# A planner's durations: float32 value products at their traced length, and rough durations without a margin from the seventeenth head on

## The chip, the cores and the metric

One core of a Trainium2 chip runs the whole kernel in one launch. The metric is the device time of that launch in microseconds (us); lower is better. The engines are called PE (TensorE), DVE (VectorE), ACT (ScalarE), POOL (GpSimd) and SP (SyncE, which here only issues DMAs).

## What is computed

Three layers stand behind each other, all with float32 results (cut from the reference):

```python
# attention: 4 batches, 8 heads, 576 positions, head size 64
scores = q @ k^T / 8 + min(bias, 0)      # bias from a running sum of max(s, 0); causal
attn   = exp(scores - max);  attn /= sum + 1e-9;  x = attn @ v      # -> 2304 tokens x 512
# first MoE-like layer (w_in, w_out are float64)
h = x @ w_in;  g = h * sigmoid(1.702 * h);  x = g @ w_out           # 512 -> 2048 -> 512
# second layer: 8 experts
P = exp(x @ w_gate - max), rows and columns of P balanced 8 times
out = sum over e of  P[:, e] * (max(x @ w1[e], 0) @ w2[e])          # 512 -> 1024 -> 512
```

## The kernel before

**Stages.** Attention and the first layer run interleaved until about 560 us, the rest of the first layer follows to about 660 us, and the second layer, eight experts over three blocks of 768 tokens, takes all that is left. The change touches what is planned in the first two stretches.

**Attention** goes through 64 heads (a head of the code is one batch, one of 8 heads and one of two ranges of its queries). Each head gives one unit (256 queries in two groups) or three units (groups of 128, 128 and 64 queries), 128 units in all. A unit takes three steps on PE, each behind work of other engines:

- `scores` (line 816): products into the tile `sp`; then DVE adds the mask and takes the least value (`sm<-sp,mask`), and ACT takes the exponential (`sm<-sm,stats`).
- `turn` (line 866): PE transposes (`tp<-ident,sm`); for the first 14 heads (`N_F`) a copy to `pf` follows, later ACT writes a float16 part `ph` and DVE the rest `pl`.
- `values` (line 893): PE multiplies with the values (`op<-vf,pf` in float32 for the first 14 heads, `op<-v,ph` and `op<-v,pl` in float16 afterwards); then `finish` on DVE.

Operands of a later head are prepared by `prep` (line 663): the load `kq`, a cast to `one`, a DMA `two<-one` inside the chip's memory, and two subtractions.

**First layer.** A token block of 256 becomes whole when its heads are finished. For each of 8 weight pairs `mm1` (line 1054) makes 24 products into `hp`, then tanh, a product and a split into `gh` and `gl` on ACT and DVE; `mm2` (line 1076) makes 24 products into `acc` (or `accx`). These are called block products below. They come in groups of 12, and a group depends on little, so it can stand between two steps of attention. The weights are float64 and are loaded (`st`) and split by `convert` (line 1168), on ACT and DVE.

**What sets the order.** Every instruction of the kernel goes through a `Sequencer` (line 61) while the program is built. It keeps a clock for each engine and gives each instruction a planned duration (`cost`, line 138), an extra time until its result counts as there (`op.tail`, in `submit`, line 159), and a time at which its inputs are ready (`depend`, line 199). PE instructions are placed at once; those of the other engines are held and issued in the order in which the planner thinks that they can run (`run`, line 259). `any_copy` (line 479) gives a copy to DVE or ACT, whichever is planned to be less loaded.

The main loop (from line 2034) asks each kind of PE work when its inputs are there (`can_vpow`, `can_flush`, `can_value`, `can_turn`, `can_score`, then the first layer), and takes the first kind in this list that is ready. It asks twice: first with `seq.slack = SLACK`, 1000 ns on top of each input's planned end (`settled`, line 101), so that a step whose inputs are only just there gives way to a block product; and if nothing passes, with 0. Where nothing is ready and the first block product hasn't come yet, `fill` (line 476) puts in products that nobody reads (`unread<-mask`), to keep PE working.

Planned durations of before, in ns, with n the columns: a matmul n / 2.4 (four times this for float32 operands) plus 2.7 or 13 and a weight load that isn't hidden; DVE 66 + n / 0.96 (60 more with a scalar operand from a tile) with a tail of 85; ACT 50 or 90 + n / 1.2 (100 more with such an operand) with a tail of 110. From `begin_second` (line 1888) on, `seq.fine` is set, and other durations hold.

All engine instructions are recorded by one helper, so the profile shows line 307 for nearly everything; tiles tell them apart. `n_pv` counts the heads whose values are prepared; `2 * H` is 16.

## Time and profile before

| | us |
|---|---|
| median of 3 runs (2004.4 to 2006.52) | 2006.13 |
| the profiled execution, its own time | 2004.02 |
| span of that execution, first to last instruction | 2002.3 |
| PE busy in the span | 1964.1 (98%) |
| DVE busy | 1471.9 (74%) |
| ACT busy | 1249.3 (62%) |
| POOL busy | 87.2 (4%) |

The chain that ended last runs through PE for 73% of the span. Busy time of PE includes products that run at the lower of its two clocks, so the granted clock (a share of full speed, by stretch) has to be read beside it. A matmul's duration in the profile has a modelled end; what one costs in a row of equal ones is the distance from start to start. A float32 product (both operands plain float32) is recorded as two matmuls.

### The profile page before, as it was taken

How to read it: one execution, taken by the hardware profiler on the slowest of the kernel's cores; microseconds unless marked ns; L12 is line 12 of the kernel's file. 1: busy time of each engine (PE TensorE's matmuls, PEld its weight loads, DVE VectorE, ACT ScalarE, POOL GpSimd, SP SyncE). 2: the span in 40 equal slices, each digit the busy share in tenths (PEclk: the TensorE clock that was granted, in tenths of full speed). 3: DMA queues.
4: the chain of work that ended last, by engine and by line, in shares of the span. 5: the costliest groups of instructions: out<-in, count | busy, mean ns of one | idle time of the engine just before them, and what ended most of it. 6: DMA issues, size and time to landing. Idle time of an engine off the chain costs nothing.

```text
span 2002.3 us, 41146 instructions
## 1 busy us (share of the span) xinstructions
PE 1964.1 (98%) x15805; PEld 1578.6 (79%) x15805; DVE 1471.9 (74%) x3421; ACT 1249.3 (62%) x2576; POOL 87.2 (4%) x144
## 2 busy tenths in 40 slices
PE   7989999999999999999999999999999999999999
PEld 6888999999998677777777777777777777777777
DVE  7787888887853676988877766776786876777656
ACT  6787667675634575666666666656666666665333
POOL 1000000000000000000000111111101001111000
PEclk9999999999999999999999999999999999999999
DMA  8455455444226454475475566667557556566331
GB/s 253 126 187 176 123 141 155 130 130 118 76 69 213 156 198 151 159 257 182 156 256 145 131 184 176 181 171 203 161 130 244 152 156 181 163 172 182 119 129 43
DMA packets 230100, 322.12 MB, mean 161 GB/s; under 512 B 38272, under 2 KB 156224, under 8 KB 229904
## 3 DMA queue, kind: packets, MB, share of 16 engines
q1 hardware_dynamic: 216944, 295.90, 45.1%
q0 software_dynamic: 12960, 23.60, 8.2%
q8 instruction: 124, 2.03, 0.4%
q14 instruction: 72, 0.59, 0.1%
HBM read 230.85 MB, written 84.34 MB: 157 GB/s over the span
## 4 chain that ended last, share of the span: by engine, by line
PE 73%; DVE 10%; ACT 6%; DMA 2%; issue 1%; SPq 0%; ACTq 0%; DVEq 0%
PE C L307 16%; PE A L307 16%; PE D L307 16%; PE B L307 8%; PE hp L307 6%; PE acc L307 3%; ACT h L307 2%; PE accw L307 2%; DVE h L307 2%; PE op L307 1%; PE sp L307 1%; PE tp L307 1%; DVE hst L307 1%; DVE sa L307 1%; DMA kq<-in_qk_dram 1%
## 5 line engine op out<-in xcount | busy, mean ns | idle before, releaser
L307 PEld LDWEIGHTS <-h 128*128 128x128 f16 x6048 | 591.4, 98 | 85.4 <-issue 6.7
L307 PEld LDWEIGHTS <-w1o 128*128 128x128 f16 x4036 | 394.6, 98 | 255.1 <-issue 4.4
L307 PE MATMUL C<-xt,w1o 128*128 128x384 f16 x1152 | 218.6, 326 | 1.4 <-DVE hst L307 1.4
L307 PE MATMUL D<-xt,w1o 128*128 128x384 f16 x1152 | 218.4, 326 | 0.0
L307 PE MATMUL D<-w2o,h 128*128 128x256 f16 x1728 | 217.7, 273 | 0.2 <-ACT y L307 0.2
L307 PE MATMUL A<-xt,w1o 128*128 128x384 f16 x1152 | 214.8, 326 | 0.1
L307 PE MATMUL A<-w2o,h 128*128 128x256 f16 x1728 | 212.2, 273 | 1.7 <-ACT B L307 1.4
L307 PE MATMUL C<-w2o,h 128*128 128x256 f16 x1728 | 208.4, 273 | 1.9 <-DVE y L307 1.7
L307 DVE SCALAR_TENSOR_TENSOR h<-hst,h 128x768 f16<-128x768 f32 (+1 forms) x192 | 139.1, 755 | 55.9 <-ACT h L307 55.9
L307 ACT COPY C<-B 128x384 f32<-128x384 f32 (+1 forms) x168 | 71.4, 425 | 154.7 <-PE B L307 93.7
L307 PE MATMUL hp<-xh,wih 128*128 128x256 f32 (+1 forms) x512 | 154.4, 302 | 0.8 <-ACT xh L307 0.5
L307 PE MATMUL hp<-xl,wih 128*128 128x256 f32 (+1 forms) x512 | 152.1, 297 | 0.6 <-DVE xl L307 0.6
L307 PE MATMUL hp<-xh,wil 128*128 128x256 f32 (+1 forms) x512 | 151.8, 297 | 0.0
L307 POOL DMA_DIRECT2D acc_d<-y x90 | 77.8, 864 | 1224.4 <-DVE y L307 660.3
L307 ACT ACTIVATE h<-hst 128x768 f16<-128x768 f32 (+1 forms) x192 | 126.2, 678 | 3.8 <-DVE hst L307 3.7
L307 ACT ACTIVATE sm<-sm,stats 64x576 f32<-64x576 f32 (+4 forms) x160 | 93.7, 602 | 41.2 <-DVE stats L307 40.1
L307 PE MATMUL acc<-gh,woh 128*128 128x256 f32 x384 | 112.4, 293 | 0.0
L307 PE MATMUL B<-w2o,h 128*128 128x256 f16 x864 | 110.5, 273 | 0.1
L307 PE MATMUL acc<-gl,woh 128*128 128x256 f32 x384 | 109.9, 286 | 0.0
L307 PE MATMUL acc<-gh,wol 128*128 128x256 f32 x384 | 109.6, 285 | 0.0
L307 PE MATMUL B<-xt,w1o 128*128 128x384 f16 x576 | 109.3, 326 | 0.0
L307 ACT COPY B<-A 128x384 f32<-128x384 f32 (+1 forms) x168 | 70.3, 426 | 59.0 <-PE A L307 58.4
(238 smaller groups left out, 3877.0 us busy)
## 6 DMA issues: line engine op xcount, KB each, us to landing
xt<-xc_d SPq DMA_DIRECT2D x168, 384.0 KB
wm<-in_moe_w_dram SPq DMA_DIRECT2D x112, 256.0 KB
w2o<-w_d SPq DMA_DIRECT2D x56, 512.0 KB
wr<-in_moe_w_dram SPq DMA_DIRECT2D x112, 256.0 KB
w_d<-wo SPq DMA_DIRECT2D x98, 256.0 KB
acc_d<-y POOLq DMA_DIRECT2D x90, 256.0 KB, 4.9
kq<-in_qk_dram SPq DMA_DIRECT2D x32, 448.0 KB
st<-in_moe_w_in_dram SPq DMA_DIRECT2D x16, 512.0 KB
```

Source lines behind the costliest of these rows:

```text
L307: self.seq.submit(self.name, what, lambda: method(*args, **named), outs, ins, "accum_op" in named)
```

## The change

It edits the planner alone; the computation stays what it is, and so do the numbers of its instructions, but for four `fill` products and a few copies that change between DVE and ACT.

- From the program's start: a float32 matmul is planned by the longer of its columns and those of its weights. The float32 value products have 65 columns and 128 (or 64) weight columns, so one goes from 4 * 65 / 2.4 + 2.7 = 111 ns to 4 * 128 / 2.4 + 10 = 223 ns. An ACT `activation` that reads bytes or a strided tile (the weight conversion) is planned 54 columns longer.
- Once `n_pv` reaches 16, `seq.rough` is set, until `seq.fine` takes over: DVE 70 + n / 0.96, ACT 90 + n / 1.2 with no addition for scalar operands, matmuls without the additions and with weight loads at nothing, float32 at 65 columns again, no tail behind DVE and ACT results, and the same waiting time behind an engine's own results as another engine would have. The main loop then asks once, with a slack of 0.
- The summary of the change names low parts on GpSimd. `any_less` (line 486), which makes the low parts, uses DVE in both versions, and GpSimd's rows are the same in both.

```diff
--- before.py
+++ after.py
@@ -79,6 +79,7 @@
         self.rank = 0
         self.holding = False
         self.fine = False
+        self.rough = False
         self.slack = 0
         self.cold, self.since, self.streamed = True, 0.0, 0.0
         self.late = 0.0
@@ -135,9 +136,25 @@
             n *= x
         return n
 
+    @staticmethod
+    def strided(ap):
+        return abs(list(ap.ap)[-1][0]) > 1
+
     def cost(self, engine, what, out, ins, sums=False):
         n = max(self.size(x) for x in [out] + ins[:2])
         psum = any(x.space == PSUM for x in ins)
+        if self.rough and not self.fine:
+            if engine == "PE":
+                n = self.size(out)
+                if what == "transpose":
+                    return 2 * n / 2.4
+                slow = ins[0].dtype == F32 or ins[0].dtype == F32R and n < 256
+                return n * (4 if slow else 1) / 2.4
+            if engine == "DVE":
+                quick = what in ("tensor_copy", "tensor_scalar") and not psum
+                return 70 + n / (1.92 if quick else 0.96)
+            if engine == "ACT":
+                return 90 + n / 1.2 + 190 * sums
         if self.fine:
             if engine == "PE":
                 return self.size(out) * (4 if ins[0].dtype == F32 else 1) / 2.4 + (13 if ins[0].dtype == F32R else 2.7)
@@ -145,13 +162,17 @@
             n = self.size(out)
             if what == "transpose":
                 return 2 * n / 2.4 + 3
-            slow = ins[0].dtype == F32 or ins[0].dtype == F32R and n < 256
+            if ins[0].dtype == F32:
+                return 4 * max(n, self.size(ins[0])) / 2.4 + 10
+            slow = ins[0].dtype == F32R and n < 256
             return n * (4 if slow else 1) / 2.4 + (13 if ins[0].dtype == F32R else 2.7)
         by = any(self.size(x) == 1 for x in ins[1:]) and n > 1
         if engine == "DVE":
             quick = what in ("tensor_copy", "tensor_scalar") and not psum
             return 66 + 60 * by + n / (1.92 if quick else 0.96)
         if engine == "ACT":
+            if what == "activation" and (ins[0].dtype == U8 or self.strided(ins[0])):
+                n += 54
             return (50 if psum else 90) + 100 * by + 93 * sums + n / 1.2
         return 80 + n * {"memset": 0.3, "tensor_scalar": 2.7}.get(what, 2.24)
 
@@ -171,9 +192,11 @@
             op.stream = 0.36 if what == "matmul" and ins[0].dtype == F32 else 1.0
             sums = len(outs) > 1
             if engine == "PE":
-                op.load = 110 if BYTES[ins[0].dtype] == 4 else 27
+                op.load = 0 if self.rough else 110 if BYTES[ins[0].dtype] == 4 else 27
             op.cost = self.cost(engine, what, outs[0], ins, sums)
-            op.tail = {"DVE": 85, "ACT": 110}.get(engine, 0) + 90 * sums
+            op.tail = 0
+            if self.fine or not self.rough:
+                op.tail = {"DVE": 85, "ACT": 110}.get(engine, 0) + 90 * sums
         for ap, writes in [(x, False) for x in ins] + [(x, True) for x in outs]:
             name = ap.tensor.name
             if name in self.outside:
@@ -200,7 +223,7 @@
         if on.end is None:
             op.waits.add(on)
             on.after.append(op)
-        elif on.engine == op.engine != "PE" and not on.nbytes:
+        elif (self.fine or not self.rough) and on.engine == op.engine != "PE" and not on.nbytes:
             op.ready = max(op.ready, on.end + AFTER_OWN)
         elif on.engine != "PE" or op.engine != "PE":
             op.ready = max(op.ready, on.end + LATENCY.get((on.engine, op.engine), LATENCY.get(on.engine, 0)))
@@ -2039,7 +2062,9 @@
         more_scales()
         seq.run()
         now = seq.free["PE"]
-        for seq.slack in (SLACK, 0):
+        if not seq.rough and n_pv >= 2 * H:
+            seq.rough = True
+        for seq.slack in (0,) if seq.rough else (SLACK, 0):
             times = [can_vpow(), can_flush(), can_value(), can_turn(), can_score(), moe1_can()]
             which = next((k for k, x in enumerate(times) if x <= now), None)
         if at_first and seq.share() < SHARE:
```

The instructions move on all engines until about the end of attention; the last 10,658 matmuls of PE (the whole second layer among them) stand in the same order as before. Three places follow; `acc`, `hp`, `sp`, `tp` and `op` are the tiles named above, `vtp` a transposition for the scale of the values, which marks the same point of the program in both.

**PE at the first 8-column `vtp`**, in the last of the float32 heads (heads 11 to 13). Before, from the last block product on:

```order
L307 MATMUL acc_945<-gh,wol_79 128x256
L307 MATMUL vtp<-ident,vmax 8x128
L307 MATMUL tp<-ident,sm 128x64 x5
L307 MATMUL sp<-one_114 64x288
L307 MATMUL sp<-two_115 64x288
L307 MATMUL sp<-one_114 64x288
L307 MATMUL sp<-two_115 64x288
L307 MATMUL tp<-ident,sm 128x128 x3
L307 MATMUL op<-vf_134,pf 64x65
L307 MATMUL op<-vf_135,pf 64x65
L307 MATMUL op<-vf_136,pf 64x65
L307 MATMUL op<-vf_137,pf 64x65
```

After that the list goes on for 142 matmuls (44 transpositions, 24 of scores, 74 of values) without a block product. With the change:

```order
L330 MATMUL hp<-xh,wil_81 128x256
L330 MATMUL op<-vf_134,pf 128x65
L330 MATMUL op<-vf_135,pf 128x65
L330 MATMUL op<-vf_136,pf 128x65
L330 MATMUL op<-vf_137,pf 128x65
L330 MATMUL vtp<-ident,vmax 8x128
L330 MATMUL op<-vf_134,pf 64x65
L330 MATMUL op<-vf_135,pf 64x65
L330 MATMUL op<-vf_136,pf 64x65
L330 MATMUL op<-vf_137,pf 64x65
L330 MATMUL op<-vf_138,pf 64x65
L330 MATMUL tp<-ident,sm 128x128 x7
```

The `vtp` now stands between two groups of 12 `hp` products, with 39 matmuls of attention between the groups (15 transpositions, 8 of scores, 16 of values). In the part ahead of it, three other stretches of attention without a block product or a `fill` are 27, 31 and 37 matmuls long.

**SP's DMA queue between the `two<-one` of head 20 and that of head 21.** Before:

```order
L307 DMA two_113<-one_112 64x256
L307 DMA two_115<-aux_d 4x2x256
L307 DMA va<-in_v_dram 128x128
L307 DMA kq<-in_qk_dram 128x2x256
L307 DMA st<-in_moe_w_in_dram 128x2x512
L307 DMA st<-in_moe_w_out_dram 128x1024
L307 DMA st<-in_moe_w_in_dram 128x2x512
L307 DMA two_113<-aux_d 4x2x256
L307 DMA va<-in_v_dram 128x128
L307 DMA two_115<-one_114 64x256
```

With the change:

```order
L330 DMA two_113<-one_112 64x256
L330 DMA kq<-in_qk_dram 128x2x256
L330 DMA st<-in_moe_w_in_dram 128x2x512
L330 DMA st<-in_moe_w_out_dram 128x1024
L330 DMA two_113<-aux_d 4x2x256
L330 DMA st<-in_moe_w_in_dram 128x2x512
L330 DMA two_115<-one_114 64x256
```

Three loads of weights (`st`) stand between the two in both; two small loads that stood in front of the second `two<-one` have moved elsewhere. On PE, the block products between the last scores of head 19 and the first of head 21 go from 72 to 84, and the value products from 18 to 27. Between heads 24 and 26 the same count of block products falls from 36 to 12.

**PE between the scores and the transpositions of a unit of head 51**, at about 400 us. Before (24 `hp` products stand between):

```order
L307 MATMUL sp<-one_114 128x256
L307 MATMUL sp<-two_115 128x256
L307 MATMUL hp<-xh,wih_1592 128x256
L307 MATMUL hp<-xl,wih_1592 128x256
L307 MATMUL hp<-xh,wil_1593 128x256
...
L307 MATMUL hp<-xl,wih_1592 128x256
L307 MATMUL hp<-xh,wil_1593 128x256
L307 MATMUL tp<-ident,sm 128x128 x3
```

With the change (12 of them):

```order
L330 MATMUL sp<-one_114 128x256
L330 MATMUL sp<-two_115 128x256
L330 MATMUL hp<-xh,wih_1408 128x256
L330 MATMUL hp<-xl,wih_1408 128x256
L330 MATMUL hp<-xh,wil_1409 128x256
...
L330 MATMUL hp<-xl,wih_1408 128x256
L330 MATMUL hp<-xh,wil_1409 128x256
L330 MATMUL tp<-ident,sm 128x128 x3
```

The transposition has come closer to the scores whose exponential it reads. Among the units from 60 to 127, five now have 12 block products there, alone or with two of scores or 9 to 15 of values (1.4 to 2.0 us by the starts of equal products in the trace); before, the least of these five had 12 with 18 of values.

## Rows read from the trace of the kernel before

**Rows 1.** The page: span.

```profile
span 2002.3 us, 41146 instructions
```

**Rows 2.** Windows by stage: from:to, length, busy us (x) of PE, PEld, DVE, ACT, POOL; clock, DMA, GB/s.

```profile
35.00:190.00 155.00, 141.46 (x1206) 129.32 (x1204) 128.71 (x361) 122.90 (x235) 1.31 (x9) 0.93 0.54 166
190.00:560.00 370.00, 363.81 (x3597) 347.82 (x3596) 300.95 (x922) 244.35 (x506) 3.18 (x22) 1.00 0.45 128
560.00:2002.00 1442.00, 1432.87 (x10811) 1080.98 (x10809) 1020.99 (x2056) 861.61 (x1795) 77.80 (x90) 1.00 0.55 167
```

**Rows 3.** The same columns, windows of 5 us in the early stretch.

```profile
75.00:80.00 5.00, 3.72 (x31) 3.44 (x29) 3.96 (x12) 3.14 (x7) 0.00 (x0) 1.00 0.51 120
80.00:85.00 5.00, 5.00 (x30) 4.53 (x28) 3.47 (x9) 2.10 (x3) 0.00 (x0) 0.66 0.67 226
85.00:90.00 5.00, 4.92 (x40) 4.00 (x39) 4.32 (x20) 4.01 (x7) 0.14 (x1) 1.00 0.09 24
90.00:95.00 5.00, 5.00 (x33) 4.17 (x32) 3.46 (x11) 3.38 (x7) 0.14 (x1) 0.66 0.06 14
...
135.00:140.00 5.00, 3.68 (x21) 3.59 (x22) 2.68 (x8) 3.61 (x8) 0.00 (x0) 0.54 0.65 216
140.00:145.00 5.00, 5.00 (x40) 5.00 (x38) 4.00 (x10) 3.33 (x8) 0.00 (x0) 0.78 0.39 94
...
170.00:175.00 5.00, 4.73 (x25) 3.67 (x24) 4.50 (x10) 3.08 (x6) 0.15 (x1) 0.50 0.65 209
```

**Rows 4.** Timeline of PE: start us, us, what [idle before <-releaser].

```profile
84.22 0.29 PE L307 MATMUL acc<-gh,wol 128*128 128x256 f32 x1
...
87.98 0.88 PE L307 MATMUL op<-vf,pf 128*128 128x65 f32 x6
88.67 0.48 PE L307 MATMUL sp<-one 128*128 128x512 f32 x1
...
101.55 0.22 PE L307 MATMUL op<-v,ph 128*128 128x65 f16 x2 [0.93 <-DVE xg L307]
...
103.30 0.20 PE L307 MATMUL op<-v,pl 128*128 128x65 f16 x1 [0.69 <-DVE pl L307]
...
103.89 0.36 PE L307 MATMUL hp<-xh,wih 128*128 128x256 f32 x1
```

**Rows 5.** Waits of PE from 0 to 560 us: us in total, times, longest.

```profile
PE sp L307 <- DMA two<-one: 4.0, 3, 2.9
...
PE op L307 <- DVE pl L307: 2.3, 5, 0.7
...
PE tp L307 <- ACT sm L307: 1.7, 4, 0.9
```

**Rows 6.** Timeline of the DMA queue of SP, 127 to 131 us.

```profile
127.26 0.38 SPq L307 DMA_DIRECT2D st<-in_moe_w_in_dram  x1
...
130.63 0.52 SPq L307 DMA_DIRECT2D two<-one  x1
```

**Rows 7.** Timeline of PE, 132 to 137 us.

```profile
132.22 0.28 PE L307 MATMUL hp<-xl,wih 128*128 128x256 f32 x1
...
133.17 0.28 PE L307 MATMUL sp<-one 128*128 128x256 f32 x1
136.32 0.58 PE L307 MATMUL sp<-two 68*128 68x256 f32 x1 [2.86 <-DMA two<-one]
```

**Rows 8.** ACT by form, 190 to 560 us: xcount | busy us, mean ns | idle before.

```profile
L307 ACT ACTIVATE sm<-sm,stats 128x256 f32<-128x256 f32 x16 | 8.0, 502 | 2.9 <-DVE stats L307 2.9
...
L307 ACT ACTIVATE sm<-sm,stats 128x128 f32<-128x128 f32 x16 | 6.4, 401 | 3.2 <-DVE stats L307 3.1
L307 ACT ACTIVATE va<-va,vpow 128x128 f32<-128x128 f32 x16 | 6.2, 395 | 1.4 <-DVE vpow L307 0.8 <-DMA va<-in_v_dram 0.6
```

**Rows 9.** DVE by form, 190 to 560 us.

```profile
L307 DVE CUSTOM_DVE_ANT_0 sm<-sp,mask 128x256 f32<-128x256 f32 x16 | 6.6, 415 | 0.0
...
L307 DVE CUSTOM_DVE_ANT_0 sm<-sp,mask 128x128 f32<-128x128 f32 x16 | 4.5, 281 | 3.6 <-PE sp L307 2.6 <-PE vtp L307 0.8
```

## The prediction

> **What bounds the kernel now.** The span is 2002.3 us [rows 1]; the profiled execution took 2004.02, 1.7 more for what lies around the span, and stands 2.1 under the median of 2006.13. I read the windows by stage first [rows 2]: what TensorE lacks of a window's length is its idle time. From 35 to 190 us it is 155.0 - 141.5 = 13.5 us, from 190 to 560 us 370.0 - 363.8 = 6.2, from 560 on 1442.0 - 1432.9 = 9.1. So TensorE is the bound everywhere, and a new order of the same products can only win or lose idle time and time at the lower clock. The last 10,658 matmuls keep their order, so from about 560 us on I count nothing.
>
> Next come the windows of 5 us [rows 3]. A granted clock of 0.66 over 5 us means that 0.34 of the window was lost, 1.7 us, since the clock has only its two levels, full speed and half (2.4 and 1.2 GHz). After 35 us it falls four times: in 80 to 85 (1.7 lost), in 90 to 95 (1.7), in 135 to 145 (5 x 0.46 + 5 x 0.22 = 3.4) and from 170 on (2.5 in the window shown). From 190 us on it is at 1.00 [rows 2]. Idle and clock together put about 25 us at stake between 35 and 190 us, and 6 us after that.
>
> Two places explain much of it. From 84.22 to 103.89 us no block product runs [rows 4]; inside stand waits of 0.93 and 0.69 us, and the clock falls although TensorE had been busy for 4.92 of the 5 us before [rows 3]. At 133 us the scores of head 21 wait 2.86 us for the DMA `two<-one` [rows 7], and the clock falls behind that wait. All waits for this transfer until 560 us sum to 4.0 us, 2.9 of it here [rows 5].
>
> **The change part by part.** It removes no work from an engine that bounds. Four `fill` products fewer, copies that go to DVE in place of ACT and back, and the order of GpSimd, which stays, cost nothing: they lie beside TensorE's other work, and for a copy that comes late the price is in term F. What is left is where the products stand.
>
> *A, the stretch without block products.* The planner had a float32 value product at 111 ns; three of them, with the hand-over behind them, take from 87.98 to 88.67, 0.23 us each [rows 4]. So it had thought that the early heads leave more time for block products than they do, had spent them, and had none at 84 us. Planned at 223 ns, they are spread: 142 matmuls in a row become 39 and less. I take back the fall in 90 to 95, -1.7, and half of the two waits of 0.93 + 0.69, -0.8: together -2.5 (between 0 and -3.3).
>
> *B, falls that are new.* The three stretches of 27 to 37 matmuls ahead of that place, and the one of 39, are float32 attention as at 84 to 91 us; after about 6 us of that the clock fell. 37 matmuls at the mean of the old stretch (19.7 us less 1.6 idle and 1.7 for the clock, by 142, is 0.115 us) are 4.3 us, with 17 value products at 0.23 rather 6. So one of them may lose the clock, +1.7 (between 0 and, for three, +5.1).
>
> *C, 75 to 85 us.* Idle 5.00 - 3.72 = 1.28 and a fall of 1.7 [rows 3]. The order here is another, and what it waits for isn't settled by it; I take half, -1.5 (between 0 and -3.0).
>
> *D, the wait of head 21.* Between the last scores of head 19, which free the operand's slot, and the scores of head 21, twelve block products and nine value products more. A block product costs 0.119 us from start to start: eight from 132.22 to 133.17 [rows 7]. With 0.3 for the value products that is 1.7 us more cover for a wait of 2.86. The clock lost 3.4 behind it; half of that goes if the wait is 1.2 us. Sum -3.4 (between 0 and -6.3). On SP, three loads still stand ahead of the transfer. The row shows that it was issued at 130.63, 3.4 us behind the last load [rows 6], and that the product that needed it began at 136.32 [rows 7], 5.7 us later.
>
> The Trainium skill, page "DMA: Bandwidth & Descriptors", section "Two DMAs through the same engine are not ordered", says that the descriptors of one queue start in order on a DMA engine, though they may end in another. By this rule the three loads delay the transfer as before and D is nothing; the trace agrees as far as 5.7 us for so small a transfer goes.
>
> *E, head 26.* Its cover falls from 36 block products to 12, 24 x 0.119 = 2.9 us less. Its transfer then needs to land earlier than it had to; a wait of the kind of rows 7 may come up here. Between 0 and +4.6 (2.9 and one fall of 1.7); I take +1.0, since the waits of this kind other than head 21's come to 4.0 - 2.9 = 1.1 us in all [rows 5].
>
> *F, no margin from 190 to 560 us.* With a slack of 0 and no tails, attention is put in as soon as the plan says that its inputs are there. ACT is planned short: `va<-va,vpow` over 128 columns is 90 + 128 / 1.2 = 197 ns in the rough plan and 395 in the trace, an exponential the same 197 against 401 [rows 8]. Matmuls are planned short too, 107 ns against 119, which gives ACT and DVE some of that time back. In the order, five units have only about 1.4 to 2.0 us of products between scores and transpositions; for a unit of two groups the chain there is 0.28 + 0.42 on DVE [rows 9] and 0.50 on ACT [rows 8], 1.2 us, and the hand-overs between three engines. Where the old order came out short, a wait cost 1.7 / 4 = 0.4 for transpositions and 2.3 / 5 = 0.5 for value products [rows 5]. Five at 0.45 are +2.2 (between 0, if the hand-overs fit, and +5 at a us each).
>
> The fall at 170 us stays in the sum as it is: its attention is still a long stretch without block products in the new order.
>
> Sum: -2.5 + 1.7 - 1.5 - 3.4 + 1.0 + 2.2 = -2.5. On the profiled execution 2001.5; on the median **2003.6 us**. The low ends sum to -12.6, the high ends to +14.7.
>
> **The rivals.** *1, more is won.* Head 21's wait goes whole with its fall (-6.3), C whole (-3.0), A whole (-3.3), one new fall (+1.7), E and F hidden: -10.9, **1995.2**. For it: after 190 us TensorE hardly ever waited. Against: each of these waits ends a chain on other engines that are as busy as before.
>
> *2, slower: the margin was needed.* Place: transpositions waiting for the exponential, value products waiting for `pl`, from 190 to 560 us. Idle there is 6.2 in 370, 1.7%; where the order had little to choose, from 35 to 190, it is 13.5 in 155, 8.7% [rows 2]. Half way between is 5.2%, 19.3 us, +13.1 in place of F's 2.2; with the other terms (-4.7) the sum is +8.4, **2014.5**. For it: ACT's rough durations are half of the traced ones for short work, and the plan no longer sees when it is behind. Against it: between most steps stand over 2.2 us of products, and block products are plentiful until the end of attention. It decides once idle from 190 to 560 us passes 6.2 + 4.7 + 4 = 15 us.
>
> *3, head 21 still waits.* The three loads stand in front as before, so the wait and the clock stay: D is 0 and the sum +0.9, **2007.0**. It is what the skill's rule on one queue comes to here.
>
> That the change does only part of what it says is certain for GpSimd, which never made low parts; that part is worth 0 in all cases.
>
> **How the numbers follow.** About 0.2%, 4 us, is what a measurement can tell from no change. Forecast 0.50, with a range of its own of 1999 to 2008: of that I give 0.16 to faster by over 4 us (under 2002.1) and 0.34 to no change. Rival 1 has 0.18, all faster; rival 2 0.24, all slower; rival 3 0.08, no change. That makes faster 0.34, same 0.42, slower 0.24. The range goes from rival 1's time to just under rival 2's, 1995 to 2014, which leaves out half of each, 0.09 and 0.12.
>
> **What would show it.** In the profile of the changed kernel: no window of 5 us between 85 and 105 us with block products absent throughout, and fewer than four falls of the clock after 35 us (A, B); idle from 35 to 190 us under 13.5 us; waits for `two<-one` under 4.0 us with the longest under 2 us (D, E); idle from 190 to 560 us between 6 and 11 us, with more on exponentials and `pl` (F); 560 us to the end the same within 1 us. The prediction is wrong if idle after 190 us passes 15 us, or if the clock falls where it had not fallen before, after 190 us, or if the second layer changes its time although its order is the same.

## The result and the profile after

| | before | after |
|---|---|---|
| median of 4 runs, us | 2006.33 (2004.4 to 2007.08) | 1987.35 (1985.29 to 1989.53) |
| ratio, 95% interval | | 0.9909 [0.9892, 0.9927] |
| span of the profiled execution | 2002.3 | 1983.2 |

The change saves 19.0 us, 0.9%. The forecast was 2003.6, the range ended at 1995: the sign was right, the size more than seven times too small (-2.5 against -19.0), and the time lies 7.7 us below the range.

The page of after, its span and the busy times (share of the span, instructions). PE is now busy 99% of the span:

```profile
span 1983.2 us, 41145 instructions
...
PE 1958.3 (99%) x15801; PEld 1573.7 (79%) x15801; DVE 1471.7 (74%) x3420; ACT 1249.4 (63%) x2577; POOL 87.5 (4%) x144
```

Windows by stage of after, columns as in [rows 2]:

```profile
0.00:35.00 35.00, 27.83 (x198) 22.35 (x199) 22.84 (x82) 19.84 (x40) 4.95 (x23) 0.85 0.85 253
35.00:190.00 155.00, 149.04 (x1338) 138.14 (x1336) 135.87 (x386) 130.41 (x250) 1.46 (x10) 0.98 0.58 180
190.00:560.00 370.00, 368.32 (x3617) 351.28 (x3616) 292.51 (x891) 239.84 (x494) 3.06 (x21) 1.00 0.41 118
560.00:1983.00 1423.00, 1413.12 (x10656) 1061.91 (x10654) 1020.51 (x2064) 859.34 (x1794) 78.04 (x90) 1.00 0.57 170
```

The row of before that rows 2 left out:

```profile
0.00:35.00 35.00, 25.92 (x200) 20.45 (x201) 21.27 (x86) 20.49 (x42) 4.94 (x23) 0.95 0.86 255
```

Read as in the prediction: idle time is the length of a window less PE's busy time; the clock's loss is added up over windows of 5 us, each 5 us times the missing share.

| stage, us | idle before, after | lost to the clock before, after | sum of the two |
|---|---|---|---|
| 0 to 35 | 9.1, 7.2 | 1.7, 5.2 | +1.6 |
| 35 to 190 | 13.5, 6.0 | 10.2, 3.4 | -14.3 |
| 190 to 560 | 6.2, 1.7 | 0, 0 | -4.5 |
| 560 to the end | 9.1, 9.9 | 0, 0 | +0.8 |

Both columns come from one execution of each kernel, and the clock's is not the kernel's own. Over 56 executions of before that ran beside the experiments, the mean granted clock goes from 0.990 to 0.997 and the time goes with it, from 2009.9 us (the mean of the four at 0.990) to 2002.0 (the two at 0.997). So a second measure is used below: the span times its granted clock, an estimate of the time without the clock's losses (the clock is known to 0.001, which is 2 us). It is 1990.4 us for before, the mean of the 56, and 1973.4 for after, the mean of 4: about 17 of the 19 us were not won from the clock.

The table comes to -16.4 of the span's -19.1 us. The rest, some 2.7 us, is busy time at the full clock; what it is wasn't settled. By the trace `accw`, the last part of the first layer, starts at 582.6 us before and at 562.8 after, and from there to the end it takes 1419.7 and 1420.4 us: the second layer, whose order is the same, takes the same time, and all of the gain lies ahead of it.

Windows of 5 us of after, those in which the clock falls with the ones ahead of them, and three of the places that the prediction spoke of (75 to 85, 90 to 95 and 130 to 140 us):

```profile
5.00:10.00 5.00, 3.16 (x13) 1.62 (x11) 0.55 (x2) 0.00 (x0) 0.61 (x4) 0.91 0.75 147
10.00:15.00 5.00, 5.00 (x21) 4.00 (x20) 3.65 (x17) 3.57 (x9) 0.00 (x0) 0.50 1.14 305
...
25.00:30.00 5.00, 2.88 (x26) 2.47 (x24) 3.46 (x15) 3.50 (x8) 0.00 (x0) 0.96 1.04 393
30.00:35.00 5.00, 4.91 (x54) 4.58 (x53) 4.96 (x14) 3.71 (x6) 0.14 (x1) 0.70 0.99 345
35.00:40.00 5.00, 3.46 (x21) 2.10 (x18) 4.94 (x19) 3.87 (x8) 0.00 (x0) 0.99 0.93 295
40.00:45.00 5.00, 4.99 (x40) 4.55 (x40) 4.32 (x13) 4.41 (x9) 0.00 (x0) 0.67 0.76 266
...
75.00:80.00 5.00, 5.00 (x45) 4.37 (x44) 4.96 (x13) 3.46 (x7) 0.14 (x1) 1.00 0.61 187
80.00:85.00 5.00, 4.67 (x37) 3.88 (x36) 4.37 (x21) 3.15 (x5) 0.00 (x0) 1.00 0.61 181
...
90.00:95.00 5.00, 5.00 (x50) 4.62 (x49) 4.77 (x15) 3.57 (x8) 0.15 (x1) 1.00 0.07 16
...
130.00:135.00 5.00, 5.00 (x51) 4.96 (x50) 4.96 (x16) 5.00 (x12) 0.00 (x0) 1.00 0.73 240
135.00:140.00 5.00, 5.00 (x50) 4.95 (x49) 4.86 (x16) 4.98 (x12) 0.00 (x0) 1.00 0.75 232
160.00:165.00 5.00, 3.50 (x38) 2.29 (x37) 4.69 (x13) 3.64 (x9) 0.02 (x1) 1.00 0.87 283
165.00:170.00 5.00, 3.94 (x21) 3.39 (x21) 4.89 (x11) 4.49 (x9) 0.00 (x0) 0.66 0.39 127
```

The falls at 80, 91 and 135 us [rows 3] are gone, the one at 170 us has become one of 1.7 us (165 to 170), and there are new ones before 45 us (whether these are the change's own is asked further below). Every fall of after stands behind a stretch in which PE was idle: 1.84 us of 5 to 10, 2.12 of 25 to 30, 1.54 of 35 to 40, 1.50 of 160 to 165.

PE's waits in after from 0 to 560 us (total, times, longest), against [rows 5]: `two<-one` goes from 4.0 to 0.4, `pl` from 2.3 to 0.8, and the transpositions that waited 1.7 us for the exponential are no longer listed.

```profile
PE sp L330 <- DVE stats L330: 2.2, 3, 1.1
...
PE op L330 <- DVE pl L330: 0.8, 3, 0.3
PE sp L330 <- DMA two<-one: 0.4, 1, 0.4
```

Timeline of PE at the scores of head 21 in after, which [rows 7] showed with a wait of 2.86 us; no wait stands beside them:

```profile
130.71 0.19 PE L330 MATMUL op<-v,pl 128*128 128x65 f16 x1
130.74 0.36 PE L330 MATMUL sp<-one 128*128 128x256 f32 x1
130.94 0.28 PE L330 MATMUL sp<-two 68*128 68x256 f32 x1
```

And the transfer for them on the DMA queue of SP in after, the last load of weights in front of it included:

```profile
124.73 0.38 SPq L330 DMA_DIRECT2D st<-in_moe_w_in_dram  x1
126.47 0.52 SPq L330 DMA_DIRECT2D two<-one  x1
```

**A mistake in the description ahead of the prediction.** The main loop asks with a slack of 1000 ns and then with 0, and the second pass was said to count only if nothing passes in the first. The `break` that should end the search stands behind a `continue`, inside the condition for `fill`, where it is never reached. So the pass with 0 decided always, in both kernels, and the line of the change that leaves the first pass out changes nothing. The margin of 1000 ns that the change was thought to take away had never been there; the tails of 85 and 110 ns had been.

### The profile page after: what moved, and what is told of

Same layout as the page of the kernel before. It is cut to its first block, busy times and chain, and to the rows that moved or that the text cites. A ratio compares the mean times of both kernels' runs of the same rounds, so it can differ in the third digit from the quotient of the medians.

```text
span 1983.2 us, 41145 instructions
## 1 busy us (share of the span) xinstructions
PE 1958.3 (99%) x15801; PEld 1573.7 (79%) x15801; DVE 1471.7 (74%) x3420; ACT 1249.4 (63%) x2577; POOL 87.5 (4%) x144
## 4 chain that ended last, share of the span: by engine, by line
PE 84%; DVE 7%; ACT 5%; DMA 2%; issue 1%; SPq 0%; ACTq 0%; DVEq 0%
PE C L330 16%; PE A L330 16%; PE D L330 16%; PE hp L330 9%; PE B L330 8%; PE acc L330 6%; PE sp L330 3%; PE op L330 3%; PE tp L330 2%; ACT h L330 2%; PE accw L330 2%; DVE h L330 2%; PE accx L330 1%; DVE hst L330 1%; DVE sa L330 1%
```

## The experiments

The change has two halves: the value products' cost with the 54 columns for conversions ("value cost"), and the rough mode from the 16th prepared head on. The rough mode has three parts: products planned short, DVE and ACT planned short, no tails. Theories: **R** (rival 2), less of a margin costs waits, and the value cost wins; **P**, the short products are what wins, since they leave every chain on DVE and ACT more real time than the plan thinks; **N**, any new order wins or loses some tenths of a per cent by chance. The expectations below were written with numbers: theory 1 is the value cost, theory 2 the rough durations, theory 3 is N, theory 4 is P, and theory 5 says that the rough mode only works as a whole. No experiment changes the computation. All results, with idle time and clock losses worked out as above from one profiled execution each; a ratio is to executions of before next to that kernel's own, and the last column is the span times its granted clock, the mean of all executions of the kernel:

| kernel | median, us | ratio to before, 95% | idle 35-190 | idle 190-560 | clock 0-35, 35-190, 190-560 | span x clock |
|---|---|---|---|---|---|---|
| before | 2006.33 | | 13.5 | 6.2 | 1.7, 10.2, 0 | 1990.4 |
| after | 1987.35 | 0.9909 [0.9892, 0.9927] | 6.0 | 1.7 | 5.2, 3.4, 0 | 1973.4 |
| e1_value_cost | 1994.87 | 0.9933 [0.9915, 0.9951] | 7.7 | 7.2 | 6.8, 0, 0 | 1985.5 |
| e2_rough_only | 1993.32 | 0.9929 [0.9912, 0.9946] | 10.2 | 2.5 | 1.7, 1.7, 0 | 1984.5 |
| e6_no_tails | 1998.75 | 0.9962 [0.9945, 0.9978] | 9.5 | 9.3 | 3.4, 0, 1.7 | 1987.7 |
| x2_va_rough | 1998.93 | 0.9954 [0.9935, 0.9972] | 8.7 | 7.2 | 5.1, 5.2, 0 | 1985.2 |
| x4_products_as_before | 2005.54 | 0.9998 [0.9985, 1.001] | 7.6 | 13.2 | 5.1, 3.5, 1.7 | 1993.1 |
| c1_before_dve70 | 2000.8 | 0.998 [0.9969, 0.9991] | 12.0 | 5.1 | 3.4, 6.8, 0 | 1986.5 |
| c2_before_lat140 | 1998.72 | 0.9962 [0.9948, 0.9975] | 13.3 | 6.9 | 8.5, 3.4, 0 | 1987.8 |
| c6_after_dve66 | 1993.3 | 0.9933 [0.9915, 0.9952] | 8.7 | 2.3 | 3.4, 5.1, 0 | 1976.7 |
| h_89 | 1984.52 | 0.9886 [0.9866, 0.9907] | 6.2 | 1.5 | 5.2, 1.7, 0 | 1975.3 |
| h_108 | 2015.93 | 1.0049 [1.0035, 1.0063] | 9.3 | 17.1 | 6.1, 5.9, 5.1 | 2002.8 |
| f1_before_margin | 2005.32 | 0.9995 [0.9983, 1.0007] | 12.7 | 12.2 | 6.8, 8.6, 1.7 | 1986.4 |
| z1_fills | 1986.7 | 0.9902 [0.9878, 0.9926] | 4.0 | 5.4 | 3.4, 1.7, 0 | 1977.4 |
| k_89 | 1986.74 | 0.9911 [0.9891, 0.9932] | 9.0 | 3.1 | 1.7, 3.4, 0 | 1978.2 |
| h_80 | 1989.19 | 0.9917 [0.9895, 0.9939] | 7.1 | 3.7 | 3.4, 5.1, 0 | 1977.8 |
| h_95 | 1987.55 | 0.9911 [0.9891, 0.9931] | 8.0 | 3.7 | 8.5, 0, 0 | 1976.7 |

Below, one row each of the windows from 190 to 560 us, in which PE's busy time is the first number behind the length, carries the verdict.

**Which half: e1 and e2.** From after, without ever setting the rough mode:

```diff
-        if not seq.rough and n_pv >= 2 * H:
-            seq.rough = True
```

> The changed kernel without its rough mode: only the float32 value products at 223 ns and the longer weight conversion stay, so the order is the changed one up to the first float16 value product (about 90 us) and is planned as before from there. Theory 1, the early order does it (block products kept in store until 95 us, so that nothing runs dry later): 1988 to 1994 us. Theory 2, the rough durations do it, from 95 us on: the two traces differ by only about 3 us at head 13, so 2001 to 2005 us. Theory 3, chance (every new order draws its dozen stalls and falls of the clock anew): anywhere from 1985 to 2012.

And from after, without the value cost:

```diff
-            if ins[0].dtype == F32:
-                return 4 * max(n, self.size(ins[0])) / 2.4 + 10
-            slow = ins[0].dtype == F32R and n < 256
+            slow = ins[0].dtype == F32 or ins[0].dtype == F32R and n < 256
...
-            if what == "activation" and (ins[0].dtype == U8 or self.strided(ins[0])):
-                n += 54
```

> The other half alone: rough mode from the seventeenth head on, but the float32 value products at 111 ns and the conversion as before, so the order is that of before up to about 95 us, with no block product left in store there. Theory 1: 2001 to 2008, the stretch without block products at 84 to 104 us and its falls stay. Theory 2: 1988 to 1993. Theory 3: anywhere, and its gain and that of the run before don't add up to the 19 us of the change.

The stage windows of e1, then of e2:

```profile
190.00:560.00 370.00, 362.78 (x3571) 346.32 (x3569) 297.39 (x911) 240.78 (x504) 3.03 (x21) 1.00 0.43 123
```

```profile
190.00:560.00 370.00, 367.46 (x3619) 350.96 (x3618) 292.43 (x881) 239.03 (x489) 3.04 (x21) 1.00 0.42 118
```

Each half alone gives about -0.7%, the two together -0.9%: they don't add up. They work in different places. The value cost takes idle time out of 35 to 190 us (13.5 to 7.7) and leaves 190 to 560 us as it was (7.2). The rough mode takes it out of 190 to 560 us (2.5). Between them the early stage splits: from 75 to 105 us, where A and C lie, idle time goes from 3.6 us in before to 0.7 in e1 and 4.3 in e2, so there it is the value cost; from 105 to 190 us it goes from 7.2 to 3.7 and 3.2, so there either half does it. That PE waits less with the whole rough mode is against R.

**Which part of the rough mode: e6, x2, x4.** With the value cost, e6 keeps every planned duration and weight load as before, so that only the tails and the shorter time behind an engine's own results go; x2 keeps the tails and the products, so that only DVE and ACT are planned short; x4 is after with the products and their loads as before.

```diff
 e6_no_tails (against after)
-        if self.rough and not self.fine:
+        if False:
...
-                op.load = 0 if self.rough else 110 if BYTES[ins[0].dtype] == 4 else 27
+                op.load = 110 if BYTES[ins[0].dtype] == 4 else 27
 x2_va_rough and x4_products_as_before (against after)
-            if engine == "PE":
-                n = self.size(out)
-                if what == "transpose":
-                    return 2 * n / 2.4
-                slow = ins[0].dtype == F32 or ins[0].dtype == F32R and n < 256
-                return n * (4 if slow else 1) / 2.4
...
-                op.load = 0 if self.rough else 110 if BYTES[ins[0].dtype] == 4 else 27
+                op.load = 110 if BYTES[ins[0].dtype] == 4 else 27
 x2_va_rough alone
-            if self.fine or not self.rough:
+            if True:
...
-        elif (self.fine or not self.rough) and on.engine == op.engine != "PE" and not on.nbytes:
+        elif on.engine == op.engine != "PE" and not on.nbytes:
```

> The changed kernel with the traced-like durations kept in rough mode: only the tails of 85 and 110 ns behind DVE and ACT and the shorter own-engine wait go, from the seventeenth head on. Theory 1: 1987 to 1994, as the early order is the changed one. Theory 2: if steps planned closer to their inputs are what helps, 1987 to 1993; if it is the short durations of the products, 2000 to 2005. Theory 3: anywhere between 1985 and 2012.

> The changed kernel with rough mode cut to the durations of DVE and ACT (no addition for scalar operands): tails, own-engine waits and the durations of PE stay as before. Theory 1: 1987 to 1994. Theory 2: 2000 to 2005 if the tails or the products matter, 1987 to 1993 if ACT's short exponentials do. Theory 3: anywhere between 1985 and 2012.

> The changed kernel with the products of PE planned as before (119 to 120 ns for a block product instead of 107, weight loads counted), all else of rough mode kept. If the short products are what makes attention run ahead, so that its steps find their inputs, idle from 190 us to the end of attention is 6 to 9 us again and the time 1993 to 2000 us. If they don't matter, 1 to 3 us of idle there and 1984 to 1990 us.

The stage windows of e6, x2 and x4, in this order:

```profile
190.00:560.00 370.00, 360.72 (x3535) 342.84 (x3534) 297.48 (x908) 239.56 (x494) 3.04 (x21) 1.00 0.43 122
```

```profile
190.00:560.00 370.00, 362.79 (x3562) 344.02 (x3561) 300.02 (x916) 241.94 (x505) 3.03 (x21) 1.00 0.43 123
```

```profile
190.00:560.00 370.00, 356.82 (x3482) 337.19 (x3482) 294.98 (x900) 240.15 (x496) 3.04 (x21) 1.00 0.42 120
```

Against e1's 7.2 us of idle time, no tails alone give 9.3, short DVE and ACT durations alone 7.2, both 13.2. So the two parts together do what R said; the 2.1 us of the first alone are no more than an edit without meaning moves (next paragraph). With the products put back the change is worth nothing (0.9998): the short products are the part that wins, and they win back what the other two lose.

**Chance: c1, c2, c6.** Three edits of a few ns that mean nothing: DVE's fixed part 66 to 70 in before, a latency of DVE 128 to 140 in before, and the rough DVE's 70 to 66 in after.

```diff
 c1_before_dve70 (against before)
-            return 66 + 60 * by + n / (1.92 if quick else 0.96)
+            return 70 + 60 * by + n / (1.92 if quick else 0.96)
 c2_before_lat140 (against before)
-    "PE": 197, "ACT": 150, "DVE": 128, "POOL": 75,
+    "PE": 197, "ACT": 150, "DVE": 140, "POOL": 75,
 c6_after_dve66 (against after)
-                return 70 + n / (1.92 if quick else 0.96)
+                return 66 + n / (1.92 if quick else 0.96)
```

> A control: the kernel before with DVE planned at 70 ns in place of 66 in its fixed part, a change that means nothing, but gives another order of the same work. If the kernel before is typical of its planner, 2003 to 2010 us with idle time and clock together costing some 20 us or more between 35 and 190 us, and about 6 us of idle time after 190. If it had drawn an unlucky order there, 1992 to 2001 us: the falls of the clock after 35 us cost under 6 us in place of 10, and idle from 190 us on stays at 5 to 9 us.

> A second control: the kernel before with results of DVE counted as there 12 ns later. Typical: 2003 to 2010 us. Unlucky before: 1992 to 2001 us, with the same signs as in the first control. If the two controls lie on different sides, order alone spreads over some 10 us.

> A control on the other side: the changed kernel with DVE's rough duration at 66 ns in place of 70. If rough mode is what cuts the waits, 1984 to 1992 us with 1 to 3 us of idle time from 190 us to the end of attention, as in the two kernels measured with all of it. If the changed kernel was a lucky draw, 1993 to 2003 us and idle there at 5 to 9 us.

Both versions of before came out faster than before, by 0.2 and 0.4%. That of after has a ratio of 0.9933 where after has 0.9909; the intervals overlap. So N is true for a part. How much of it is the order and how much the clock of the execution? By the last column c1 and c2 are 3.3 and 2.0 us below the executions of before next to them (1989.8), and c6 is 3.3 above after: an edit that means nothing moves the order's own time by 2 to 4 us, and the rest is clock. Idle time from 190 to 560 us moves too: 5.1 and 6.9 beside before's 6.2, 2.3 beside after's 1.7, and 5.4 in z1 below, which plans that stretch by the same durations as after. So up to some 4 us there can be chance, 13.2 and 17.1 beside 7.2 are not.

**The scale of the products: h_89, h_108, then h_80, h_95, k_89.** If P holds, one factor on the planned products, with tails, DVE and ACT as before, must do what the rough mode does, and a factor over one the opposite. The factor is put into e1 and, for k_89, into before, which has no value cost:

```diff
+            if engine == "PE" and self.rough and not self.fine:
+                op.cost *= 0.89
...
+        seq.rough = n_pv >= 2 * H and n_fin < len(heads)
```

> The kernel with the value cost alone (1994.9 us, 7.2 us idle from 190 us on) and one thing added: from the seventeenth head to the end of attention each product of PE is planned at 0.89 of its length (a block product at 106 ns in place of 119), with tails and the durations of DVE and ACT as before. Theory 4 (products planned short act as a margin: the plan's DVE and ACT get more real time for each product than it thinks): idle from 190 us to the end of attention falls to 1 to 3 us, total 1986 to 1992 us. Theory 5 (rough mode acts as a whole, the products are not enough): idle there stays at 5 us or more, total 1992 to 2002 us.

> The same with products planned at 1.08 of their length (129 ns). Theory 4: attention steps are put in before their inputs are there, idle from 190 us on rises from 7 us to 10 us or more, total 1998 to 2008 us. Theory 5: no trend, idle at 5 to 9 us, total 1990 to 2000 us.

> Value cost and products at 0.95. Theory 4 with a smooth course between 1.00 (7.2 us idle after 190 us) and 0.89 (1.5 us): idle 3 to 5.5 us, total 1987 to 1994 us. With an edge: idle near 1.5 or near 7.

> Value cost and products at 0.80. If more of this margin goes on helping: idle after 190 us under 1.5 us and 1980 to 1985 us. If it has all been had at 0.89 and attention then only falls behind: idle between 0.5 and 3 us, but falls of the clock or more block products missing later, 1984 to 1992 us.

> The kernel before and nothing but the products planned at 0.89 from the seventeenth head to the end of attention, without the value cost. Theory 4: idle from 190 us to the end of attention 1 to 3 us in place of 6.2, and the time near that of the whole rough mode without the value cost (1993 us): 1988 to 1996 us. If the value cost is needed as well: idle there over 4 us and 1997 to 2005 us.

The stage windows of h_108, h_95, h_89, h_80 and k_89, in this order (e1 above is 1.00):

```profile
190.00:560.00 370.00, 352.89 (x3423) 332.21 (x3422) 292.26 (x891) 234.34 (x484) 3.08 (x22) 0.99 0.42 118
```

```profile
190.00:560.00 370.00, 366.32 (x3626) 349.54 (x3625) 302.01 (x922) 247.50 (x515) 3.19 (x22) 1.00 0.43 124
```

```profile
190.00:560.00 370.00, 368.47 (x3623) 351.85 (x3621) 301.45 (x920) 243.62 (x507) 3.08 (x22) 1.00 0.43 121
```

```profile
190.00:560.00 370.00, 366.28 (x3627) 351.67 (x3626) 299.27 (x907) 243.80 (x504) 3.03 (x21) 1.00 0.41 118
```

```profile
190.00:560.00 370.00, 366.87 (x3629) 350.62 (x3628) 298.31 (x905) 240.56 (x496) 3.03 (x21) 1.00 0.41 119
```

Idle time by factor: 17.1 us at 1.08, 7.2 at 1.00, 3.7 at 0.95, 1.5 at 0.89, 3.7 at 0.80. It goes the way that P says, down to 0.89. The course below that isn't one of the products: `array` (line 239) plans a product to start no sooner than its weight load of 110 ns allows, and the factor leaves the load as it is. A row of block products is therefore planned at 129, 120, 114, 110 and again 110 ns each, so h_89 and h_80 have nearly the same plan, the expected "106 ns" is 110, and the 2.2 us between the two are of the size of chance. In after the load is planned at nothing, and a block product takes 107. The last column has the same course: 2002.8, 1985.5, 1976.7, 1975.3, 1977.8 us. The longest wait in h_108 is that of a value product for `xg`, a DVE result, 2.8 us; in h_89 none passes 0.3 us after 190 us. PE's waits from 190 to 560 us, the first rows of h_108 and of h_89:

```profile
PE op L332 <- DVE xg L332: 4.7, 3, 2.8
PE op L332 <- DVE stats L332: 2.4, 5, 0.8
```

```profile
PE op L332 <- DVE stats L332: 1.3, 5, 0.3
```

The real margin can be counted in the traces. In how many units after 190 us does the value product start less than 0.3 us behind the end of the copy `pl` that it reads? In h_108 25, before 21, e1 16, h_95 12, h_89 8, k_89 5, h_80 3, after 3, but in x4 22. The count falls with the planned product; x4 has the products of before, and copies that are planned too short. Chance moves it as well: counted the same way, c1 has 14 and c2 13, with the products of before.

k_89, one factor on the order of before, gives 0.9911: alone it makes all of the change's gain in time, and by the last column 12 of its 17 us. The best ratio was that of h_89, the value cost with the factor, 0.9886. Its interval overlaps that of after, and by the last column after is lower, so that it beats after isn't shown.

**A margin at the question: f1.** The `break` of before moved to where it works, so that a step must have 1000 ns to spare or nothing else must be ready.

```diff
+            if which is not None:
+                break
         if at_first and seq.share() < SHARE:
             fill(128)
             continue
-            if which is not None:
-                break
```

> The kernel before with its margin brought to life: the break that should end the search with a slack of 1000 ns stands behind a continue, so that the pass with 0 always decides; here it stands in the loop. If a margin is what the old plan lacked (theory 4 in another form): idle from 190 us on 1 to 3 us in place of 6.2, total 1990 to 1999 us. If the margin holds attention back instead: steps come late, block products run out, idle before 190 us rises, total 2005 to 2020 us.

The stage window of f1:

```profile
190.00:560.00 370.00, 357.76 (x3552) 342.38 (x3551) 298.53 (x913) 244.30 (x503) 3.20 (x22) 1.00 0.45 127
```

Nothing is won (0.9995), and idle time grows from 6.2 to 12.2 us. A margin of 1000 ns when a step is chosen isn't the margin that a shorter planned product gives: in f1 the value product of only one unit starts within 0.3 us of its copy, but the steps wait for other results of DVE (`stats` 4.4 us, `xg` 4.0).

**The early clock: z1.** After loses 5.2 us to the clock in the first 35 us, before 1.7. The edit counts a float32 value product at half in the planner's count of PE's activity, which calls for `fill` products, and lets a step of the values' scales in 1.5 us before its input.

```diff
-            op.stream = 0.36 if what == "matmul" and ins[0].dtype == F32 else 1.0
+            op.stream = (0.18 if self.size(outs[0]) < 128 else 0.36) if what == "matmul" and ins[0].dtype == F32 else 1.0
...
-        elif seq.settled(first_of.tensor.name) > seq.free["PE"]:
+        elif seq.settled(first_of.tensor.name) > seq.free["PE"] + 1500:
```

> The changed kernel with the float32 value products counted at half in the share that decides on fill products, so that fills are again as many as a cost of 111 ns gave, 150 in all (and the early scale steps offered 1.5 us sooner, without which the planner doesn't come to its end). If the falls of the clock in the first 35 us, 5.1 us lost in the changed kernel and 1.7 before, come from too few fills: 1.7 us lost there, total 1982 to 1986 us. If not, 1985 to 1993 us, as any other order of it.

3.4 us are still lost there, and 5.4 us of idle time stand after 190 us; the total is that of after (0.9902). But the test misses its aim: the trace has 150 `fill` products in place of 118, and of these 92 lie in the first 35 us, where after has 93. The other kernels say more. After and the nine kernels that take its value cost and change something later (e1, e6, x2, x4, c6 and the four h) issue the same instructions in the same order on every engine up to about 90 us, and their executions lose 3.4 to 8.5 us to the clock in the first 35. Before, e2 and k_89 share their order up to about 92 us, and c2 shares it up to 64; they lose 1.7, 1.7, 1.7 and 8.5. So these losses change from execution to execution at the same order. What sets them stays open.

## Why the prediction was wrong

**The step that failed is F**, "No margin from 190 to 560 us", +2.2 (0 to +5); it measured -4.5. The prediction saw both effects and put them in one sentence each: short ACT durations cost waits, and matmuls "are planned short too, 107 ns against 119, which gives ACT and DVE some of that time back". It counted the first and let the second pass as a remark. The experiments show their sizes: short copies and no tails cost 13.2 - 7.2 = 6.0 us of idle time (x4 against e1), short products win them back and 5.5 more (after, 1.7). That is one execution each; the eight kernels with short products have 1.5 to 5.4 us there, the nine others 5.1 to 17.1. Why the second effect is the larger was not tested by itself; the account that fits is this. A duration that is planned 10% short on the engine that bounds works on every chain of the other engines at once, since the plan measures their time in products: 24 block products, thought to be 2.6 us, pass in 2.9. The 204 ns by which an exponential is planned short (197 against 401 [rows 8]) work once per step. And F's first premise, that a slack of 0 is new, was false: the pass with 1000 ns is dead code in both kernels.

**A** (-2.5, 0 to -3.3): right, at its bound. 90 to 95 us is at 1.00 with PE busy 5.00, so the fall of 1.7 and the two waits of 1.6 us went together. The idle time is the value cost's (75 to 105 us: 0.7 in e1, 4.3 in e2). The fall is partly luck: e2 and k_89 have before's order there, and neither falls from 90 to 95 us.

**B** (+1.7, 0 to +5.1): at its bound, and for another reason. After loses 3.5 us more than before in the first 35 us and 1.7 in 40 to 45, 5.2 together. But these falls stand behind idle time of PE at 5 to 10, 25 to 30 and 35 to 40 us, not in the long stretches of float32 attention that the prediction pointed to. Nor are they shown to be the change's: at the order of after the first 35 us lose 3.4 to 8.5 us, at that of before 1.7 to 8.5, by the execution.

**C** (-1.5, 0 to -3.0): whole. 75 to 80 us lost its 1.28 us of idle time (there PE is busy 5.00 us in after) and 80 to 85 its fall. Of the three executions with before's order, before and k_89 fall there and e2 doesn't, so this part, too, is one of chance.

**D** (-3.4, 0 to -6.3): whole, -6.3. The cover from head 19's last scores to head 21's grew as thought (122.2 to 133.5, 11.3 us before; 117.5 to 130.9, 13.4 us after: +2.1 where 1.7 was estimated). What the prediction held fixed was the 5.7 us from the transfer's issue to the product. In after the product starts 4.5 us behind the issue and doesn't wait, so the transfer took 4.5 us at most, with the same three loads in front. Rival 3, and with it what the Trainium skill's page "DMA: Bandwidth & Descriptors", section "Two DMAs through the same engine are not ordered", came to here, is refuted as a price: with descriptors that start in order behind three loads, the product still didn't wait. That the loads delay the transfer isn't refuted, since 4.5 us is only a bound on its time in after. Nor had the last load more time: it was issued 3.4 us ahead of the transfer before [rows 6], 1.7 us ahead of it in after. What the prediction didn't count is the loads further ahead: in the 8.7 us in front of the transfer before issued five loads of weights, after three. That this made it land sooner isn't shown. Either half of the change is enough: the longest wait for `two<-one` from 35 to 560 us is 0.3 us in e1 and in e2, and 2.8 in c2.

**E** (+1.0): nothing. All waits for `two<-one` come to 0.4 us, and these lie at 36 us.

**The fall at 170 us**, held in the sum as it was, is half as long: -1.7.

The forecast, then, took halves where the wholes came: A to E with the fall at 170 us measure -3.3 in A, -3.0 in C, -6.3 in D and -1.7, less the +5.2 of B: -9.1 against the forecast's -4.7 (the table has -12.7 from 0 to 190 us, so 3.6 us of idle time went in places that no term named). Of the -12.7 the clock's share is -3.3 us in these two executions; in the mean of all executions the clock gives back 1.6 us. With -4.5 for F in place of +2.2 the terms come to -13.6 against -2.5. Rival 1, "more is won", had A, C and D whole and came nearest (1995.2), with F hidden at best. Rival 2's mechanism exists: in x4 less of a margin costs waits, and h_108, past the 15 us from which it was to decide, is slower than before (17.1 us of idle time, 2015.9). In the change the short products outweigh it. The prediction's own sign that it is wrong, idle time over 15 us after 190 us, didn't come: what was missing was a bound below zero for F. The text gave "0, if the hand-overs fit" as its best end, although 6.2 us of idle time [rows 2] and waits of 1.7 and 2.3 us [rows 5] stood there to be won.

**How much of it is the change's own?** From 190 us on, the gain belongs to the short products: shown by the factor's series, by x4 and by k_89. The span times clock agrees for the whole: 1973.4 to 1984.5 us for the eight kernels with short products, 1985.2 to 2002.8 for the nine others. From 35 to 190 us, the eleven kernels with the value cost lie at 4.0 to 9.5 us of idle time and the six without it at 9.0 to 13.5, the lowest two of the six being those with short products, e2 and k_89. So both halves act there, the value cost alone from 75 to 105 us (3.6 us before, 0.7 in e1; but c1, an edit that means nothing, has 1.6). The two don't simply add: by the last column e1 is 5 us below before, e2 6, and both together 17; why is open. What before and after lost to the clock can't be credited to the change, since executions at the same order differ as much. Of the 17 us some 2 to 4 may be luck of the order, going by c1, c2 and c6; k_89 can't tell this apart, since it changes the order from the 16th head on too.

## What to carry to other kernels

Where a planner orders work for an engine that bounds, the scale of its planned durations there, against those of the engines that feed it, is the margin: look first whether the bound is planned short or long against the trace (107 to 119 ns here), and try a factor (block products planned at 110 ns in place of 120 took idle time from 7.2 to 1.5 us, at 129 it came to 17.1) before a margin in ns at each decision, which here gained nothing. When an edit has two effects of opposite sign, price both, and let the range of each reach past zero when there is idle time to be won. And before a new order is credited with some tenths of a per cent, run the old one with an edit that means nothing, and read the granted clock of every execution beside its time: here it went from 0.990 to 0.997 for one and the same kernel, with 8 us between the times.

## What was not expected of the hardware

From 190 to 560 us, in the one execution of each kernel that was profiled, the clock fell in four kernels alone, and they are the four with the most idle time there: e6 (9.3 us), f1 (12.2), x4 (13.2) and h_108 (17.1); with 7.2 us and less it never did. Two windows of 5 us of h_108 show one such fall, behind a value product's wait of 2.8 us:

```profile
290.00:295.00 5.00, 2.21 (x22) 1.92 (x21) 4.61 (x16) 3.50 (x9) 0.00 (x0) 1.00 0.62 184
295.00:300.00 5.00, 4.97 (x42) 4.96 (x42) 4.75 (x18) 3.41 (x12) 0.00 (x0) 0.66 0.43 124
```

PE was idle for 2.79 us of the first, and 1.7 us are lost in the second: idle time there costs more than itself. In h_108 the idle time grew by 9.9 us over e1, and the clock took 5.1 us on top. For the fall of before at 91 us, with PE busy 4.92 us of the five ahead of it [rows 3], no such idle time was found.

And the same order doesn't always meet the same clock. These are the windows of [rows 3] from 75 to 95 us in e2, which issues what before issues, in the same order on every engine, up to about 92 us; PE is as busy until 90 us, and the clock falls neither at 80 nor at 91 us:

```profile
75.00:80.00 5.00, 3.71 (x31) 3.43 (x29) 3.96 (x12) 3.23 (x6) 0.00 (x0) 1.00 0.49 142
80.00:85.00 5.00, 5.00 (x43) 4.46 (x43) 4.57 (x14) 3.31 (x5) 0.14 (x1) 1.00 0.60 204
85.00:90.00 5.00, 4.92 (x40) 4.04 (x39) 4.52 (x18) 3.87 (x8) 0.14 (x1) 1.00 0.09 23
90.00:95.00 5.00, 4.44 (x52) 3.25 (x50) 4.42 (x17) 4.22 (x9) 0.14 (x1) 1.00 0.16 41
```
